# Expert 0 of a fused attention, MoE and cosine MLP kernel: its second token batch as seven block products, and attention's pair loads, score banks and operand sums arranged anew

## The chip, the cores and the metric

The kernel runs on one core of one Trainium2 chip. The metric is the device time of one execution in microseconds (us). Three runs of the kernel before gave 1342.14 (the median), 1338.18 and 1342.61. The trace comes from a further, profiled execution.

## The reference, cut to what matters

Three stages follow each other in float32. Sliding window attention (2 batches, 8 heads, 768 tokens, 64 per head; every token sees the last 128 tokens and the first 4) gives 1536 token rows of 512. Eight experts work on all of them, weighted by a Sinkhorn balanced gate. A last MLP of 2048 hidden columns has the activation h cos h.

```python
keep = is_sink | in_window                      # 4 sink tokens, window 128
a = softmax(where(keep, q @ k.T / 8, -1e9));  x = a @ v
P = exp(x @ w_gate - max)
for _ in range(8):
    P /= P.sum(1) + 1e-9;  P /= P.sum(0) + 1e-9;  P *= N / E
for e in range(8):
    out += P[:, e:e+1] * (maximum(x @ w1[e], 0) @ w2[e])
h = out @ w_in;  return (h * cos(h)) @ w_out
```

## The kernel before

Expert work is TensorE work on split numbers: every float32 operand is kept as two float16 parts, hi and lo, and a product is three matmuls (hi hi, hi lo, lo hi) that add up in one bank of PSUM. Expert e has a first product (512 to 1024 columns, then the rectification) and a second one (1024 to 512), for token batch 0 and then for batch 1. The weights of the first product lie in `W1O`, the token operands of batch b in `XO[b]`, the rectified hidden rows in `HH`, the weights of the second product in `W2S`, the token rows (attention's result, later the output) in `ACC[b]`.

The first product has two forms. The plain form, `g1_plain` (L1099), takes the blocks as they are: 192 matmuls of 384 columns a batch, one rectification for each of 16 results. The block form, `g1` with the list `CHAIN` (L1032), works on halves of tokens and of the inner dimension with seven products in place of eight (Strassen's scheme): 168 matmuls, results added together out of the banks by DVE. It needs seven operands instead of four: sums and differences of the four weight blocks (S, on POOL, L297 to L300, split by ACT and DVE into `W1O`) and of the four token blocks. Before the change expert 0 is plain in both batches. The token sums that experts 1 to 7 need are made by `sum_operands`: from the split operands in `XO[b]`, 14 DVE steps and 4 ACT steps, for batch 0 beside expert 0's first product of batch 1, for batch 1 beside expert 1's first product.

Attention works in units: a unit is one pair of heads, one tile of 128 tokens. In turn: `scores` (L579, PE), `top` (DVE takes the maximum and brings the scores out of the bank, L589), `expo` (ACT, L599), `high` (ACT, L622), `low` (POOL, L628), `turn` (a DMA transpose on SP's queue, L638), `values` (PE, L651 and L656), `norm` (DVE, L665 to L668). For batch 0 a pair's q and k come in two halves, q as two loads of 64 rows into a zero-filled tile, so that the score matmul has 128 rows in; batch 1 has whole pairs and matmuls of 64 rows. When the token rows are there, `plain_operand` splits them (ACT hi at L176, lo at L177 on POOL or DVE) into a staging tile `xs` and a DMA transpose on SP's queue (L221) carries them into `XO[b]`, eight pieces for each batch. For batch 1 the staging tiles are two buffers in turn (the tag "f64", `bufs=2`), which the weight sums S and pieces of w2 use too.

The order is written out by hand: `put(t, every, steps)` sets steps at ticks, `run(n)` and `tick()` issue them between matmuls. On every engine instructions run in that order. PSUM has eight banks, handed out as rings by name: s for scores, x for values, l for gates and sinks, L for the plain first product, g2 for the second product. Attention runs alone at first; from `start` its steps are laid between the matmuls of expert 0's first product of batch 0 (28 ticks, `GT`), and the rest between those of its second product (24 ticks, `HT_`). The rectification for expert 0 is `act_first` (ACT the hi part, DVE the lo part straight from the bank), for the others `act_relu` (two ACT steps, then POOL).

Of the kernel before, what the change touches and what calls it, by code (L numbers as in the profile page):

```python
# [40 lines left out]
def kernel(  # L41
# [123 lines left out]
    BW = ((1, 1, 0), (0, 1, 0), (1, 0, 0), (0, 1, 0))  # L165
# [119 lines left out]
    def w1_split(e, st, js=range(NJ)):  # L285

        steps = []
        for j in js:
# [15 lines left out]
            def sp(which, j=j, by=by, ca=ca, cb=cb):  # L304
# [19 lines left out]
        return steps  # L324
# [9 lines left out]
    def attention():  # L334
# [16 lines left out]
        q0 = [xo0[:, 7 * HT * c + 3 * HT:7 * HT * c + 5 * HT] for c in range(2)]  # L351
        wide = Ring(t.rearrange("p (h w) -> p h w", h=2) for t in (q1[:, 0], q1[:, 1], *q0))
        qs = Ring([TMP.rearrange("p a b -> p (a b)")[:, 4096:4096 + S], q1[:, 0], q1[:, 1]])
        for t in wide.parts:
            for g in range(2):
                nc.vector.memset(t[64 * g:64 * g + 64, 1 - g], 0.0)
        kk = carve(2 * NT * TW)
        few = Ring(kk[:, 4 * TW * n:4 * TW * (n + 1)].rearrange("p (t w) -> p t w", w=TW) for n in (1, 2, 0))
        ks = Ring(kk[:, NT * TW * n:NT * TW * (n + 1)].rearrange("p (t w) -> p t w", w=TW) for n in range(2))
        k_sink = res.tile([128, NP, NS], F32, name="ksink")  # L360
# [21 lines left out]
        def load_qk(n, eng=nc.scalar, other=nc.scalar):  # L382
            r = order[n % NP] * 128
            if n < 2 * NP:
                half = n // NP
                t0, nt = (2, 4) if half else (0, 3)
                qk[n] = q_, k_ = wide.next(), few.next()
                eng.dma_start(
                    out=k_[:, 0:nt, 0:128],
                    in_=kT[0, r:r + 128, t0 * 128:(t0 + nt) * 128].rearrange("p (t w) -> p t w", w=128))  # L390
                for g in range(2):
# [3 lines left out]
            else:  # L395
                qk[n] = q_, k_ = qs.next(), ks.next()
                eng.dma_start(
                    out=k_[:, :, 0:128], in_=kT[1, r:r + 128, :].rearrange("p (t w) -> p t w", w=128))
                other.dma_start(out=q_, in_=qT[1, r:r + 128, :])

        def sink_cols(n):
            k_ = qk[n][1]
            if n < NP:
                nc.gpsimd.tensor_copy(out=k_sink[:, n], in_=k_[:, 0, 0:NS])
            src = k_sink[:, n % NP:n % NP + 1] if n < 2 * NP else k_[:, 0:1, 0:NS]
            a, z = ((1, 2), (0, 3), (1, NT - 1))[n // NP]
            nc.gpsimd.tensor_copy(out=k_[:, a:z, 128:TW], in_=src.to_broadcast([128, z - a, NS]))
# [138 lines left out]
        for p in range(2 * NP):  # L546
            h, p = p // NP, p % NP
            for u in range(U3):
                i = h * U3 + u
                units.append((0, p, i))  # L550
                batch.append(h * NP + p)
                sums.append((slice(h * U3, h * U3 + U3), u, U3) if p < NP - 1 else (slice(i, i + 1), 0, 1))
        for p in range(NP):
# [4 lines left out]
            for g in groups:  # L558
                tiles = range(NT)[g]
                for u, i in enumerate(tiles):  # L560
                    units.append((1, p, i))
                    batch.append(2 * NP + p)
# [3 lines left out]
        def scores(k):  # L566
# [3 lines left out]
            qi, ki = (i % U3, i - 2 * (i // U3)) if k < KB else (i, i)  # L570
            S_[k] = []
            for ab in range(2):
                sps = ring["s"].next()
                h, qh = (slice(0, 128), q_[:, ab]) if k < KB else (slice(64 * ab, 64 * ab + 64), q_)
                if sunk(i):
                    to, kh = sps[:, 0:L], k_.rearrange("p t w -> p (t w)")[h, (ki - 1) * TW:(ki - 1) * TW + L]
                else:
                    to, kh = sps[:, 0:L].rearrange("p (t w) -> p t w", w=128), k_[h, 0:i + 1, 0:128]
                nc.tensor.matmul(to, qh[h, qi * 128:(qi + 1) * 128], kh, start=True, stop=True)  # L579
# [160 lines left out]
        first = [batch.index(n) for n in range(3 * NP)]  # L740
        for n, k in enumerate(first):
            put(base(k) - 2, 1, [lambda n=n: sink_cols(n)])
            if n >= 3:
                m = n - 3 if n < 2 * NP else n - 2
                put(base(first[m + 1] - 1) + 3, 1, [lambda n=n: load_qk(n)])

        def ops(b, half, c, tiles, s0):
            def go():
                if b:
                    xs = stage.tile([128, 1536], F16, tag="f64", name="xs", bufs=2)  # L750
                else:
                    xs = xss.next()
                plain_operand(b, half, c, tiles, xs, nc.vector if c else nc.gpsimd)
# [3 lines left out]
        ends = []  # L757
        for b in range(B):
            s0 = 0
            for half in range(2):  # L760
                for c in range(2):
                    for tiles in [slice(0, U3)] if c == 0 else [slice(i, i + 1) for i in range(U3)]:
                        i = half * U3 + tiles.stop - 1
# [585 lines left out]
```

## Time and profile before

| what | us |
|---|---|
| median of three runs | 1342.14 |
| profiled execution | 1342.73 |
| its span | 1340.8 |
| PE busy in the span | 1276.2 (95%) |
| attention alone | 0 to 69.6 |
| first product of expert 0, batch 0, with attention | 69.6 to 159.5 |
| second product of batch 0, with attention's tail | 159.5 to 198.3 |
| first, then second product of batch 1 | 198.3 to 231.8, to 265.0 |
| the rest | 265.0 to 1340.8 |

The stages are bounded by the start of the first matmul of each product. A row of stretches gives for one of them its length, then busy us and number of instructions of each engine; the clock is the mean share of full speed that was granted to TensorE; the DMA share is that of the 16 engines. A waits row says which engine's instruction waited for whose, in total, how often, and the longest. A group row has the idle time ahead of the group behind the bar.

### The profile page before, as it was taken

To read this page: it belongs to the slowest core of one execution; us is meant where nothing else is said; L and a number is where in the kernel's file an instruction comes from. 1 tells how busy PE (TensorE), PEld (TensorE's weight loads), DVE (VectorE), ACT (ScalarE), POOL (GpSimd) and SP (SyncE) were. 2 spreads that over 40 slices of the span, in tenths; PEclk is the share of its full clock that TensorE was granted. 3 is DMA by queue.
4 is the path that set the end of the run, shared out by engine and by line. 5 is a ranking of instruction groups with operands and counts; after the bars stand their busy time and mean duration, and the time that the engine had idled before them with its cause. 6 is when DMAs were issued, how large, how long until landed. Compare 5 with 4: busy or idle time off the path is not lost.

```text
span 1340.8 us, 19538 instructions
## 1 busy us (share of the span) xinstructions
PE 1276.2 (95%) x7281; PEld 682.7 (51%) x7281; DVE 855.3 (64%) x1636; ACT 681.3 (51%) x1425; POOL 596.9 (45%) x742
## 2 busy tenths in 40 slices
PE   5777999999999999999999999999999998999998
PEld 4544556454555545455554545545455544445554
DVE  6675517886557554754755485475556688787674
ACT  6755632473644437164443716445372757666452
POOL 5533412150633364173336417333541857377543
PEclk7789999999999999999999999999999999999999
DMA  9998660011112310501331050132102331400001
GB/s 241 164 177 157 134 144 2 2 66 64 59 64 88 116 64 17 187 1 63 98 107 64 24 181 1 63 103 102 63 25 86 56 104 28 104 2 0 32 17 48
DMA packets 127599, 104.57 MB, mean 78 GB/s; under 512 B 89104, under 2 KB 102928, under 8 KB 127504
## 3 DMA queue, kind: packets, MB, share of 16 engines
q1 hardware_dynamic: 112384, 72.57, 21.1%
q0 software_dynamic: 7168, 25.17, 5.8%
q10 hardware_dynamic: 7952, 5.59, 1.9%
q8 instruction: 57, 0.93, 0.3%
q14 instruction: 38, 0.31, 0.1%
HBM read 70.53 MB, written 11.53 MB: 61 GB/s over the span
## 4 chain that ended last, share of the span: by engine, by line
PE 69%; DVE 9%; POOL 4%; ACT 4%; issue 3%; DMA 1%; POOLq 0%; ACTq 0%; DVEq 0%
PE bank L1116 37%; PE bank L1032 25%; PE bank L1049 4%; PE bank L1099 2%; DVE tmp L1063 1%; DVE tmp L970 1%; DMA xo<-xs 1%; DVE w2s L183 1%; POOL hh L945 1%; DVE w1o L183 1%; DVE tmp L230 1%; DVE tmp L961 1%; ACT xs L182 1%; ACT tmp L958 1%; DVE xs L183 1%
## 5 line engine op out<-in xcount | busy, mean ns | idle before, releaser
L1116 PE MATMUL bank<-w2s,hh 128*128 128x512 f16 x2880 | 637.6, 379 | 4.7 <-DVE w2s L183 2.3
L1116 PEld LDWEIGHTS <-hh 128*128 128x128 f16 x2880 | 280.9, 98 | 337.9 <-issue 6.2
L1032 PE MATMUL bank<-xo,w1o 128*128 128x384 f16 x2352 | 386.2, 326 | 0.9 <-ACT tmp L1000 0.8
L945 POOL TENSOR_TENSOR hh<-tmp,hh 128x384 f16<-128x384 f32 x224 | 206.3, 942 | 328.2 <-ACT tmp L944 319.5
L1032 PEld LDWEIGHTS <-w1o 128*128 128x128 f16 x2352 | 229.5, 98 | 154.3 <-issue 2.0
L1000 ACT ACTIVATE tmp<-bank 128x384 f32<-128x384 f32 x168 | 81.6, 487 | 289.0 <-PE bank L1032 289.0
L1004 DVE TENSOR_TENSOR tmp<-bank,tmp 128x384 f32<-128x384 f32 x168 | 91.1, 554 | 163.9 <-ACT tmp L1000 121.8
L1049 PE MATMUL bank<-xo,w1o 128*128 128x384 f16 x672 | 120.0, 329 | 6.7 <-ACT tmp L1071 3.6
L1188 DVE SCALAR_TENSOR_TENSOR acc<-bank,PS,acc 128x512 f32<-128x512 f32 x84 | 62.9, 749 | 75.9 <-PE bank L1116 75.4
L1049 PEld LDWEIGHTS <-w1o 128*128 128x128 f16 x672 | 65.9, 98 | 57.9 <-issue 10.5
L944 ACT ACTIVATE tmp<-tmp 128x384 f32<-128x384 f32 x168 | 87.9, 523 | 5.3
L943 ACT ACTIVATE hh<-tmp 128x384 f16<-128x384 f32 x168 | 86.5, 515 | 5.1 <-DVE tmp L1004 5.0
L972 POOL TENSOR_SCALAR hh<-tmp 128x384 f16<-128x384 f32 x64 | 45.7, 715 | 82.8 <-DVE tmp L970 72.9
L160 DVE TENSOR_REDUCE wm<-st 128x1 f32<-128x1024 f32 x68 | 81.7, 1208 | 0.0
L628 POOL TENSOR_TENSOR parts<-xo,parts 128x512 f16<-128x512 f32 (+1 forms) x38 | 47.4, 1249 | 71.6 <-ACT parts L622 56.7
L182 ACT ACTIVATE w1o<-S,s 128x1024 f16<-128x1024 f32 x36 | 41.2, 1145 | 74.4 <-POOL S L300 74.4
L1099 PE MATMUL bank<-xo,w1o 128*128 128x384 f16 x384 | 73.3, 341 | 1.9 <-DVE hh L950 1.9
L183 DVE SCALAR_TENSOR_TENSOR w1o<-st,s,w1o 128x512 f16<-128x512 f32 x72 | 65.1, 935 | 13.5 <-ACT w1o L182 13.4
L974 POOL TENSOR_TENSOR hh<-tmp,hh 128x384 f16<-128x384 f32 x64 | 68.8, 1076 | 5.3
L183 DVE SCALAR_TENSOR_TENSOR w2s<-st,s,w2s 128x512 f16<-128x512 f32 x72 | 60.9, 860 | 15.6 <-ACT w2s L182 15.5
L1063 DVE TENSOR_TENSOR tmp<-bank,tmp 128x384 f32<-128x384 f32 x112 | 59.2, 548 | 10.9 <-PE bank L1049 6.9
L183 DVE SCALAR_TENSOR_TENSOR w1o<-S,s,w1o 128x1024 f16<-128x1024 f32 x36 | 49.4, 1373 | 19.1 <-ACT w1o L182 19.0
(181 smaller groups left out, 1361.1 us busy)
## 6 DMA issues: line engine op xcount, KB each, us to landing
st<-in_moe_w_dram SPq DMA_DIRECT2D x56, 512.0 KB, 5.9
f<-in_moe_w_in_dram POOLq DMA_DIRECT2D x16, 512.0 KB, 4.4
f<-in_moe_w_out_dram POOLq DMA_DIRECT2D x16, 512.0 KB, 4.2
w2p<-in_moe_w_dram SPq DMA_DIRECT2D x8, 512.0 KB, 4.4
w_in<-x POOLq DMA_DIRECT2D x16, 256.0 KB, 4.3
w_out<-x POOLq DMA_DIRECT2D x16, 256.0 KB, 4.1
st<-w_out SPq DMA_DIRECT2D x8, 512.0 KB, 5.9
st<-w_in SPq DMA_DIRECT2D x8, 512.0 KB, 6.9
```

What stands on the lines that cost most here:

```text
L160: nc.vector.tensor_reduce(out=dst, in_=src, axis=axis, op=ALU.max, apply_absolute_value=True)
L183: late.append(lambda: nc.vector.scalar_tensor_tensor(out=lo, in0=src, scalar=s, in1=hi, op0=ALU.mult, op1=ALU.subtract))
L943: nc.scalar.activation(out=hi, in_=src, func=AF.Relu)
L944: nc.scalar.activation(out=dst, in_=src, func=AF.Relu)
L945: nc.gpsimd.tensor_tensor(out=lo, in0=dst, in1=hi, op=ALU.subtract)
L1000: nc.scalar.activation(out=t, in_=ps, func=AF.Copy)
L1004: nc.vector.tensor_tensor(out=t, in0=ps, in1=t, op=ALU.add)
L1032: nc.tensor.matmul(ps, W1O[:, j0 + c, wi, o, kk, :], XO[b][:, kk, o, xi, :], start=(n == 0 and o in (0, 5, 1)), stop=(n == 5), skip_group_ ...
L1049: nc.tensor.matmul(ps, W1O[:, j, wi, o, kk, :], XO[b][:, kk, o, xi, :], start=(n == 0), stop=(n == 5))
L1063: nc.vector.tensor_tensor(out=t, in0=x, in1=y, op=ALU.add)
L1099: nc.tensor.matmul(ps, W1O[:, j, wi, o, kk, :], XO[b][:, kk, x, xi, :], start=(kk == 0 and m == 0 and p == 0), stop=(kk == 1 and m == 1 an ...
L1116: nc.tensor.matmul(ps, HH[:, t // U3, hi, f, (t % U3) * 128:(t % U3 + 1) * 128], w[:, wi, f, :], start=(f == order[0] and n == 0), stop=(f ...
```

## The change

The second batch of expert 0 takes the block form (`if e == b == 0` keeps the plain form for the first batch only). For that its token operands are made by `x_operand` in six pieces of 14 blocks each, with sums T on POOL, and expert 0's weight sums S are added in the second product of batch 0 (`put(GT + 1, 1.5, w1_rest[9:])`); `sum_operands(1)` goes, and `sum_operands(0)` moves there too. The rectification is `act_relu` throughout. Batch 0's pairs are loaded whole, all at the start, and have 64 row scores. From eight ticks ahead of the first product's start, scores have four banks, values and gates one each.

```diff
-    BW = ((1, 1, 0), (0, 1, 0), (1, 0, 0), (0, 1, 0))
+    BW = ((0, 0, 0),) * 4
...
-                elif e == 0:
+                elif e == 0 and which == 2:
                     split(hi[:, 3], lo[:, 3], t[:, 0:2, cb], s, by=by[2])
...
             steps += [lambda w=w, sp=sp: sp(w) for w in range(3)]
-        return steps
+            if e == 0:
+                rest += [sums, lambda sp=sp: sp(3)]
+        return steps + rest
...
-            if n < 2 * NP:
-                half = n // NP
-                t0, nt = (2, 4) if half else (0, 3)
-                qk[n] = q_, k_ = wide.next(), few.next()
...
-                for g in range(2):
-                    other.dma_start(
-                        out=q_[64 * g:64 * g + 64, g],
-                        in_=qT[0, r + 64 * g:r + 64 * g + 64, half * HT:(half + 1) * HT])
...
+            b, r = n // NP, order[n % NP] * 128
+            qk[n] = q_, k_ = qs[n], ks[n]
+            eng.dma_start(
+                out=k_[:, :, 0:128], in_=kT[b, r:r + 128, :].rearrange("p (t w) -> p t w", w=128))
+            other.dma_start(out=q_, in_=qT[b, r:r + 128, :])
...
+        for p in range(2, NP):
+            load_qk(p, nc.sync, nc.sync)
...
-                h, qh = (slice(0, 128), q_[:, ab]) if k < KB else (slice(64 * ab, 64 * ab + 64), q_)
+                h = slice(64 * ab, 64 * ab + 64)
...
-            ops = ((0, 0), (1, 2)) if i < U3 else ((5, 0), (6, 2))
+            ops = ((0, 0), (1, 2)) if i < U3 else ((6, 2), (0, 0), (3, 0)) if b else ((5, 0), (6, 2))
...
+        def sum_ops(c, i, s0):
+            box = []
+            put(s0, 1, [lambda: box.append(x_operand(1, c, i, None))])
+            put(s0 + 2, 1, [lambda: box.pop()()])
+
+        for c in range(2):
+            for i in range(U3):
+                last = KB + (2 * c + 2) * NT - 1 - (2 * (U3 - 1 - i) if c else 0)
+                s0 = max(s0 + 3, turned[last] + 2, base(len(units)) + 6)
+                sum_ops(c, i, s0)
...
-                banks(s=(0, 1))
+                banks(s=(0, 1, 5, 7), x=(4,), l=(6,))
...
-            if e == 0:
+            if e == b == 0:
                 for half in range(2):
                     g1_plain(b, half, act)
...
+        put(GT, 1, [lambda: banks(s=(0, 1, 2, 3))])
...
-        put(6, 1, w1_rest[6:])
-        pairs = [TMP[:, n:n + 2] for n in (9, 11)]
+        put(6, 1, w1_rest[6:9])
+        put(GT + 1, 1.5, w1_rest[9:])
+        ring["c"] = Ring(W1O[:, j, wi, 4:7].rearrange("p a k w -> p (a k w)").bitcast(F32) for j in range(NJ) for wi in range(2))
+        a = ACC[0].rearrange("p t c -> p (t c)")
+        put(GT + 1, 0.75, sum_operands(0, ...))
...
-                    put(4, 2.5, sum_operands(0, *pairs))
-                if e == 1 and not b:
-                    banks(A0=(2,), A1=(3,), B0=(6,), B1=(0,), C=(1,))
-                    put(2, 2.5, sum_operands(1, *pairs))
+                    banks(A0=(2,), A1=(3,), B0=(6,), B1=(0,), C=(1,), l=(5,))
+                    ring["c"] = Ring(TMP[:, n] for n in range(9))
                 so = None
-                act = act_relu if e else act_first
+                act = act_relu
```

`x_operand(b, c, i, s)`, which the last MLP uses already, makes one piece (token tile i of both halves, every second block of columns from c):

```python
T  = stage.tile([128, 4, 128], F32, tag="z", name="T")
xs = stage.tile([128, 7, 2, 128], F16, tag="f64", name="xs", bufs=2)
g.tensor_tensor(out=T[:, 1::2], in0=x[:, 1], in1=x[:, :, 0], op=ALU.subtract)   # POOL, L197
g.tensor_tensor(out=T[:, 2], in0=x[:, 1, 1], in1=T[:, 1], op=ALU.subtract)      # L198
g.tensor_tensor(out=T[:, 0], in0=x[:, 0, 1], in1=T[:, 2], op=ALU.subtract)      # L199
split(xs[:, 0:2, 0], xs[:, 0:2, 1], x[:, 0], s)                                 # ACT hi, DVE lo
split(xs[:, 6, 0], xs[:, 6, 1], x[:, 1, 1], s)
# two steps later: ACT hi and POOL lo of T into xs[:, 2:6], then the DMA transpose of xs into XO[b]
```

On POOL, the second product of expert 0's batch 0 ended like this before: the last low parts of attention (`parts`), two low parts of token pieces (`xs`), and then the weight sums of expert 1.

```order
L628 TENSOR_TENSOR parts_111<-xo1_70,parts_111 128x512
L631 TENSOR_TENSOR parts_111<-xo1_70,parts_111 128x8
L177 TENSOR_TENSOR xs_2062<-acc1_75,xs_2062 128x2x384
L177 TENSOR_TENSOR xs_2166<-acc1_75,xs_2166 128x2x384
L297 TENSOR_TENSOR S_2655<-st_2219 128x256
```

Now the same stage has between two low parts of token pieces the sums T of a later piece, and here the four instructions of one of expert 0's weight sums.

```order
L177 TENSOR_TENSOR xs_2137<-T_2136,xs_2137 128x4x128
L197 TENSOR_TENSOR T_2179<-acc1_75 128x2x128
L198 TENSOR_TENSOR T_2179<-acc1_75,T_2179 128x128
L199 TENSOR_TENSOR T_2179<-acc1_75,T_2179 128x128
L297 TENSOR_TENSOR S_2188<-tmp_77 128x256
L298 TENSOR_TENSOR S_2188<-S_2188,tmp_77 128x256
L299 TENSOR_TENSOR S_2188<-tmp_77 128x256
L300 TENSOR_TENSOR S_2188<-tmp_77,S_2188 128x256
L177 TENSOR_TENSOR xs_2180<-T_2179,xs_2180 128x4x128
L197 TENSOR_TENSOR T_2200<-acc1_75 128x2x128
```

The third low part (`xs_2180`) stands behind the fourth sum S (`S_2188`); the numbers at the names tell one tile of a buffer from the next. On ACT, in the same stage, before: the hi parts of the eight pieces (L176), and the copies of the second product's results out of the banks (L1183).

```order
L176 ACTIVATE xs_2062<-acc1_75 128x2x384
L1183 ACTIVATE acc0_74<-bank7_85 128x512
L176 ACTIVATE xs_2097<-acc1_75 128x2x128
L176 ACTIVATE xs_2121<-acc1_75 128x2x128
L176 ACTIVATE xs_2149<-acc1_75 128x2x128
L1183 ACTIVATE acc0_74<-bank5_83 128x512
L176 ACTIVATE xs_2166<-acc1_75 128x2x384
L176 ACTIVATE xs_2176<-acc1_75 128x2x128
L176 ACTIVATE xs_2183<-acc1_75 128x2x128
L176 ACTIVATE xs_2190<-acc1_75 128x2x128
L1183 ACTIVATE acc0_74<-bank7_85 128x512
```

Now, for the last three pieces:

```order
L176 ACTIVATE xs_2201<-acc1_75 128x2x128
L176 ACTIVATE xs_2201<-acc1_75 128x128
L182 ACTIVATE w1o_71<-S_2188,s_422 128x1024
L1168 ACTIVATE acc0_74<-bank5_83 128x512
L176 ACTIVATE xs_2201<-T_2200 128x4x128
L176 ACTIVATE xs_2237<-acc1_75 128x2x128
L176 ACTIVATE xs_2237<-acc1_75 128x128
L241 ACTIVATE xo0_69<-acc0_74 128x2x384
L176 ACTIVATE xs_2237<-T_2236 128x4x128
L176 ACTIVATE xs_2257<-acc1_75 128x2x128
L176 ACTIVATE xs_2257<-acc1_75 128x128
L1168 ACTIVATE acc0_74<-bank7_85 128x512
```

Each piece has three hi parts instead of one, and the copies out of the banks (now L1168) stand between those of one piece and the next. On SP's queue the start was this before, with q and k of batch 0 in halves:

```order
L392 DMA xo_70<-in_q_dram 64x384 x2
L411 DMA acc_75<-in_v_dram 128x6x128
L388 DMA xo_70<-in_k_dram 128x3x128
L392 DMA xo_70<-in_q_dram 64x384 x2
L411 DMA acc_75<-in_v_dram 128x6x128
L388 DMA xo_70<-in_k_dram 128x3x128
L392 DMA xo_69<-in_q_dram 64x384 x2
L411 DMA acc_75<-in_v_dram 128x6x128 x2
L268 DMA tmp<-in_moe_w_dram 128x1024 x2
L638 DMA_TRANSPOSE parts<-parts 128x4x128
```

Now:

```order
L385 DMA xo_70<-in_q_dram 128x768
L394 DMA acc_75<-in_v_dram 128x6x128 x2
L383 DMA xo_70<-in_k_dram 128x6x128
L385 DMA xo_70<-in_q_dram 128x768
L394 DMA acc_75<-in_v_dram 128x6x128 x2
L383 DMA xo_69<-in_k_dram 128x6x128
L385 DMA xo_69<-in_q_dram 128x768
L383 DMA xo_69<-in_k_dram 128x6x128
L385 DMA xo_69<-in_q_dram 128x768
L268 DMA tmp<-in_moe_w_dram 128x1024 x2
L621 DMA_TRANSPOSE parts<-parts 128x4x128
```

All four pairs stand whole ahead of expert 0's w1 (`tmp`) and of attention's first transpose.

## Rows read from the trace of the kernel before

**Rows 1.** Stretches: length, busy of PE, PEld, DVE, ACT, POOL, clock, DMA, GB/s.
```profile
0.00:69.60 69.60, 44.17 (x293) 34.02 (x294) 43.57 (x171) 48.88 (x137) 36.73 (x91) 0.75 1.02 200
69.60:159.50 89.90, 70.43 (x654) 42.66 (x653) 56.03 (x176) 51.30 (x141) 35.03 (x44) 0.91 0.82 165
159.50:198.30 38.80, 38.00 (x276) 19.21 (x274) 10.93 (x35) 15.11 (x35) 10.74 (x11) 1.00 0.57 114
198.30:231.80 33.50, 33.39 (x268) 20.84 (x266) 22.04 (x37) 9.79 (x19) 6.90 (x8) 1.00 0.07 28
231.80:265.00 33.20, 32.32 (x160) 15.41 (x158) 28.98 (x83) 12.19 (x19) 5.67 (x8) 1.00 0.00 1
265.00:1340.80 1075.80, 1057.88 (x5639) 550.59 (x5637) 693.77 (x1136) 544.06 (x1075) 501.84 (x580) 1.00 0.21 65
```

**Rows 2.** Waits, 69.6 to 159.5: us in total, times, longest.
```profile
PE bank L579 <- DVE mx L589: 10.3, 5, 2.9
...
ACT parts L622 <- DMA parts<-parts: 7.1, 2, 3.7
...
PE bank L656 <- DVE acc L668: 4.0, 2, 2.1
```

**Rows 3.** Groups by line and form, DVE, 69.6 to 159.5.
```profile
L950 DVE SCALAR_TENSOR_TENSOR hh<-bank,hh 128x384 f16<-128x384 f32 x15 | 8.3, 554 | 15.1 <-ACT hh L949 15.0
```

**Rows 4.** The timeline of PE, scores: start, us, engine, line.
```profile
66.60 1.12 PE L579 MATMUL bank<-xo,xo 128*128 128x260 f32 x4
...
166.20 0.71 PE L579 MATMUL bank<-xo,tmp 64*128 64x260 f32 x4
```

**Rows 5.** DMA issues: times, KB each, median us to landing.
```profile
xo<-xs SPq DMA_TRANSPOSE x20, 4.0
```

**Rows 6.** The timeline of POOL, ACT and PE, 173 to 200.
```profile
172.27 1.16 POOL L628 TENSOR_TENSOR parts<-xo,parts 128x512 f16<-128x512 f32 x1 [0.29 <-ACT parts L622]
...
189.94 0.94 ACT L176 ACTIVATE xs<-acc 128x256 f16<-128x256 f32 x2 [4.26 <-DMA xo<-xs]
190.79 0.58 ACT L1183 ACTIVATE acc<-bank 128x512 f32<-128x512 f32 x1
...
198.15 1.14 PE L1099 MATMUL bank<-xo,w1o 128*128 128x384 f16 x6
199.12 0.45 PE L681 MATMUL bank<-wg,xo 128*128 128x8 f16 x12
```

**Rows 7.** Groups by line and form, first 370 us.
```profile
L182 ACT ACTIVATE w1o<-S,s 128x1024 f16<-128x1024 f32 x6 | 6.8, 1136 | 0.0
...
L298 POOL TENSOR_TENSOR S<-S,st 128x256 f32<-128x256 f32 x7 | 5.7, 819 | 0.5
L300 POOL TENSOR_TENSOR S<-st,S 128x256 f32<-128x256 f32 x6 | 5.6, 926 | 0.0
L297 POOL TENSOR_TENSOR S<-st 128x256 f32<-128x256 f32 x7 | 5.5, 786 | 61.7 <-DVE cr L836 41.4 <-DMA st<-in_moe_w_dram 17.4 <-DVE w1o L183 2.8
...
L299 POOL TENSOR_TENSOR S<-st 128x256 f32<-128x256 f32 x7 | 5.1, 724 | 0.0
```

**Rows 8.** Groups by line and form, whole span.
```profile
L197 POOL TENSOR_TENSOR T<-acc 128x256 f32<-128x256 f32 x12 | 10.5, 873 | 11.2 <-DVE acc L1188 6.9 <-DVE xs L183 4.2
...
L182 ACT ACTIVATE xs<-T,s 128x512 f16<-128x512 f32 x12 | 8.6, 715 | 7.8 <-POOL T L199 7.8
...
L198 POOL TENSOR_TENSOR T<-acc,T 128x128 f32<-128x128 f32 x12 | 6.4, 536 | 0.9
...
L199 POOL TENSOR_TENSOR T<-acc,T 128x128 f32<-128x128 f32 x12 | 5.8, 486 | 0.9
```

**Rows 9.** The timeline of DVE and POOL.
```profile
203.85 1.20 DVE L230 TENSOR_TENSOR tmp<-xo 128x768 f32<-128x768 f16 x1
...
204.31 1.32 POOL L298 TENSOR_TENSOR S<-S,st 128x256 f32<-128x256 f32 x1
...
208.47 0.73 POOL L298 TENSOR_TENSOR S<-S,st 128x256 f32<-128x256 f32 x1
```

More of the change, by code (lines that the diff above doesn't have):

```diff
@@ L285, in w1_split @@
     def w1_split(e, st, js=range(NJ)):
-        steps = []
+        steps, rest = [], []
         for j in js:
@@ L739, in attention @@
                 put(turned[k] + 1, 1, [lambda k=k: norm(k)])
-        first = [batch.index(n) for n in range(3 * NP)]
-        for n, k in enumerate(first):
+        for n in range(B * NP):
+            k = batch.index(n)
             put(base(k) - 2, 1, [lambda n=n: sink_cols(n)])
[L743 to L747, printed above, removed]
+            if n >= NP:
+                free = max(j for j, m in enumerate(batch) if m == (n - NP if n < NP + 2 else n - 2))
+                put(base(free) + 3, 1, [lambda n=n: load_qk(n)])
@@ L748, in go, with ops @@
+        def ops(half, c, tiles, s0):
             def go():
[L749 to L753, printed above, removed]
-            put(s0, 1, [go])
[L757 to L763, printed above, removed]
-                        last = units.index((b, 2 * c + 1, i))
-                        s0 = max(s0 + 2, turned[last] + 2, base(len(units)) + 6 if b else 0)
-                        ops(b, half, c, tiles, s0)
-                ends.append(s0 + 4)
+                plain_operand(0, half, c, tiles, xss.next(), nc.vector if c else nc.gpsimd)
+            put(s0, 1, [go])
@@ new lines, in attention @@
+        ends, s0 = [], 0
+        for half in range(2):
+            for c in range(2):
+                for tiles in [slice(0, U3)] if c == 0 else [slice(i, i + 1) for i in range(U3)]:
+                    last = units.index((0, 2 * c + 1, half * U3 + tiles.stop - 1))
+                    s0 = max(s0 + 2, turned[last] + 2)
+                    ops(half, c, tiles, s0)
+            ends.append(s0 + 4)
+        def sum_ops(c, i, s0):
+            box = []
+            put(s0, 1, [lambda: box.append(x_operand(1, c, i, None))])
+            put(s0 + 2, 1, [lambda: box.pop()()])
@@ L768, in attention @@
+        for c in range(2):
+            for i in range(U3):
+                last = KB + (2 * c + 2) * NT - 1 - (2 * (U3 - 1 - i) if c else 0)
+                s0 = max(s0 + 3, turned[last] + 2, base(len(units)) + 6)
+                sum_ops(c, i, s0)
+        ends.append(s0 + 5)
         st = {}
@@ L797, in attention @@
             if n == ends[0] - 8:
-                banks(s=(0, 1))
+                banks(s=(0, 1, 5, 7), x=(4,), l=(6,))
             run(n)
-        steps = [lambda n=n: run(n) for n in range(start, ends[3])]
+        steps = [lambda n=n: run(n) for n in range(start, ends[2])]
         k = max(0, ends[1] - 8 - start)
         def less(f=steps[k]):
-            banks(x=(4,), l=(6,))
             a16s.parts[3:] = []
@@ L945, in act_relu @@
             nc.gpsimd.tensor_tensor(out=lo, in0=dst, in1=hi, op=ALU.subtract)
-        def act_first(src, ft, half):
-            hi, lo = (HH[:, half, hl, ft] for hl in range(2))
-            nc.scalar.activation(out=hi, in_=src, func=AF.Relu)
-            nc.vector.scalar_tensor_tensor(out=lo, in0=src, scalar=0.0, in1=hi, op0=ALU.max, op1=ALU.subtract)
         def act_cos(src, ft, half, sc):
@@ L1105, in g1_plain @@
                         tick()
-                pend.append((None, lambda ps=ps, f=NJ * high + j: act(ps, f, half)))
+                pend.append((None, lambda ps=ps, f=NJ * high + j: act(ps, f, half, ring["c"].next())))
         orders = ([0, NJ, 1, NJ + 1, NJ + 2, NJ + 3, 2, 3], [f for j in range(NJ) for f in (j, NJ + j)])
@@ L1170, in layers @@
                 late = order[-1:]
-            for t in tiles if 0 < e < E else range(NT):
+            for t in tiles if 0 < e + b and e < E else range(NT):
                 if t in ps:
```

63 lines of the change are left out of this document (24 added, 39 removed).

## The prediction, made before the changed kernel ran

> **What bounds the kernel now.** I read the stretches first [rows 1]. There the reader is to set PE's busy time against the length of each stage. From 159.5 us on PE is hardly ever idle: 38.00 of 38.80, 33.39 of 33.50, 32.32 of 33.20, then 1057.88 of 1075.80. There only fewer or shorter matmuls help, or a new wait hurts. Ahead of that attention sets the pace. In the first stage PE is busy for 44.17 of 69.60 us, its clock is 0.75 of full, and the DMA engines have a share of 1.02, so nothing more fits into them. In the second, PE is busy for 70.43 of 89.90 us, at 0.91. So the change can win in the first two stages and by matmuls that go, and it can lose where the third stage hands over to the fourth.
>
> The waits of the second stage [rows 2] then show what ends PE's idle time: the score banks that DVE has not read out yet (10.3 us in 5 waits) and the value bank (4.0 us in 2). ACT's hi parts wait 7.1 us for transposes out of the tiles that they are to write, in 2 waits. The last views were groups and timelines, for prices.
>
> **The change part by part.** A, the start. 24 units of batch 0 get score matmuls with 64 rows in: a unit took 1.12 us for four matmuls with 128 rows and 0.71 with 64, both in stretches of full clock [rows 4]. If every one were on the path, 24 x 0.41 = 9.8 us would go. The memsets of DVE and five of ACT's groups of load issues go too. Against this, all four pairs now stand ahead of expert 0's w1 and the first transpose on SP's queue. With tiles of 128x768 float32 (0.39 MB), six halves of pairs move ahead there by some 1.7 MB in all; at the stage's 200 GB/s [rows 1] that is 8.6 us during which a queue that is already full serves loads which nobody needs yet. As the bytes of the whole stage are about the same and the DMA share is 1.02, I take a gain of 3 us, from -10 to +6.
>
> The Trainium skill (TensorE: Matmul & The Clock Gate, Part 3: Packing small matmuls) says that matmuls in different row groups of the array run beside each other, so a pair of 64-row score matmuls should cost about what one does, 1.12/2 = 0.56 us. The trace has 0.71, some of the way [rows 4]; by the page's rule A would be 24 x 0.15 = 3.6 us better at most.
>
> B, the first product of batch 0. Four score banks remove most of the 10.3 us [rows 2], and about half of it reappears at the next thing that is late: the transposes for which ACT already waits 7.1 us. That is -5. The single value bank can add what that wait is now, 4.0 again; as the values come later than DVE's steps I take +3. DVE loses the lo parts of the rectification, 15 x 554 ns = 8.3 us [rows 3], which were in the same queue as the score steps: -3. ACT gets a second rectification each time and POOL the subtraction; both have room (51.30 and 35.03 of 89.90). A clock of 0.91 over 89.9 us means 2 x 0.09 x 89.9 = 16 us at the lower of its two levels (1.2 of 2.4 GHz), in which 8 us are lost; with fewer holes I take -3 of these. Together -8, from -15 (all of the 10.3, the 3 and some of the clock) to 0.
>
> C, the second product of batch 0: here I see the cost. G is the start of this stage, 159.5. Before, POOL's last low part of attention ends at 173.43, G + 13.9 [rows 6]. Now POOL has these ahead of the first piece's low part: two weight sums S between attention's low parts (each four instructions, 786 + 819 + 724 + 926 ns = 3.25 us [rows 7]), of whose 6.5 us I let half vanish in POOL's idle time (it is busy for 10.74 of 38.80 [rows 1]); the sum T (873 + 536 + 486 ns = 1.9 us [rows 8]); a third S, 3.25; and the low part itself, 1.16 like the row at 172.27. So the first piece is staged at G + 13.9 + 3.2 + 1.9 + 3.25 + 1.16 = G + 23.4.
>
> From there a chain runs through two buffers: xs and S use one tag with two buffers in turn (S0, xs0, xs1, S3, xs4 in one; S1, S2, xs2, xs3, xs5 in the other, in the order in which the program asks for them). Whoever takes a buffer in which an xs lay waits until its transpose has landed, 4.0 us (20 of them, median [rows 5]). Before, eight pieces went through the same two buffers, but without S and with one hi step of ACT each; the row at 189.94 shows ACT waiting 4.26 us for just such a landing. Now the steps are: xs0 lands, 4.0. Then the hi parts of xs1 (0.94/2 = 0.47 for 256 columns and half of that for 128, 0.71), the hi part of S2 that stands between (1.14 [rows 7]), that of T (0.72 [rows 8]), the low part on POOL (1.16): 3.7. xs1 lands, 4.0. S3 may then start, and POOL has the low part of xs2 behind it: 3.25 + 1.16 = 4.4. xs2 lands, 4.0. xs3: 0.71, the hi part of S3 1.14, a copy out of a bank 0.58 [rows 6], T 0.72, low 1.16: 4.3. It lands, 4.0. xs5, which needs xs3's buffer: 0.71 + 0.58 + 0.72 + 1.16 = 3.2, and 4.0 to land. The sum is 5 x 4.0 + 15.6 = 35.6 us, so `XO[1]` is whole at G + 59.0. The block product of batch 1 starts with a product that needs all three tiles and both column blocks, so PE can begin it only there. Before it began at 198.15, G + 38.7 [rows 6]. PE waits 20 us.
>
> The bounds: if the waits for landings overlap with the work entirely, POOL alone sets it: five further pieces of 1.9 + 1.16, S3's 3.25 and one landing after G + 23.4, which is G + 45.9; with all of S0 to S2 in idle time 3 less, some +4 us. Above, every low part and sum by a quarter longer beside DVE's steps gives +26. I take +20, because each step of the chain is an order that the program fixes.
>
> What is queued behind: the copies out of banks 5 and 7 stand on ACT between the hi parts, so the second product's last two tiles wait for banks too; that lies inside the same 20 us. After so long a hole PE begins again at the lower clock: the first two stages, with their holes, are those with a clock under 1 [rows 1]. I take +1.5, from 0 to 3.
>
> D, matmuls. 192 become 168 in the first product of batch 1. Six took 0.97 us from 198.15 to 199.12 [rows 6], so 24 save 24 x 0.162 = 3.9. Gates of three tiles take 18 more small ones, 0.45/12 each, 0.7. -3.2, with little doubt: from 231.8 on the block form already runs back to back.
>
> E, operand sums. Those of batch 1 leave expert 1, those of batch 0 leave expert 0's batch 1; in the stretch 231.80 to 265.00 PE had 0.88 us idle [rows 1] and DVE was busy for 28.98. I take -2, from -3 to 0. That is what they cost now; in their new place DVE is busy for 10.93 of 38.80, and 14 steps of about 1.2 us [rows 9] go in.
>
> The sum on the profiled execution, 1342.7 (its span is 1340.8): -3 - 8 + 20 + 1.5 - 3.2 - 2 = +5.3, so 1348. This execution lies 0.6 above the median of the three runs, which are 4.4 apart; I leave it at that. A difference of 0.3%, 4 us, is about what can be told from no change.
>
> **The rivals.** R1, the chain is no chain: S and the transposes overlap, the buffers turn at POOL's pace. Then C is +4 and there is no clock to win back: -3 - 8 + 4 - 3.2 - 2 = -12, so 1331. It decides from the point where a landing holds the next piece up by under 1 us instead of 4. For it: POOL is idle most of the stage. Against it: the row at 189.94, where ACT waited for a landing with the same two buffers.
>
> R2, slower by more: attention gains nothing, since DMA sets the first stage and the pairs ahead of w1 delay it. It decides when the first transpose leaves over 5 us later than before. A is +4, B -1, the rest as forecast: 4 - 1 + 20 + 1.5 - 3.2 - 2 = +19, so 1362. For it the DMA share of 1.02 [rows 1]; against it that bytes only move within the stage.
>
> R3, DVE holds POOL up. A sum on POOL took 1.32 us while DVE's 1.20 us step with two operands from SBUF ran, and 0.73 us without [rows 9]. In C 14 such DVE steps now run beside some 22 of POOL's steps; if eight on the chain lose 0.6 each it is 5 us more, 1353. The Trainium skill (SBUF — State Buffer, Who interferes with whom) has this as a rule: the two engines share one pair of ports, and one that loses waits for the other's whole instruction. The trace agrees, with 0.6 us.
>
> R4, half of the chain holds: C is +11, 1339. A variant between forecast and R1, if the program's buffers turn in another order than I read.
>
> **How the numbers follow.** The forecast 1348, with 1340 to 1357 for its own unknowns (B alone has 7 us each way), has 0.45. R1 has 0.22, R2 0.13, R3 0.10, R4 0.10. From 1330 to 1360 holds R1's centre, R3, R4 and nearly all of the forecast; a part of R1 below and of R2 above is left out, 2 in 10. Faster than 1338.1: R1, 0.22, a third of R4 and 0.03 of the forecast, 0.29. Slower than 1346.2: R2 and R3, 0.23, and 0.31 of the forecast, 0.54. The rest, 0.17, is within 0.3%.
>
> **What would show it.** A: the first matmul of expert 0 (69.6 before) some us earlier, and the first transpose not over 5 us later. B: 82 us from there to the second product, few waits for score banks. C: a hole of PE ahead of batch 1's first block product of 15 to 25 us, ended by transposes of xs, with POOL's S3 and ACT's hi parts waiting for landings of about 4 us one after the other. D: the first product of batch 1 takes 30 instead of 33.5 us. If the hole is under 8 us the forecast is wrong in C, and the time lies near R1; if the first stage is not shorter, A and R2 decide.

## The result, and the profile after

The changed kernel took 1356.79 us (median of five runs, 1354.04 to 1357.2), against 1340.17 for the kernel before in the same session; the ratio is 1.0109, interval 1.0097 to 1.0121. It is slower: by 14.6 us by the ratio, which is not the quotient of these two medians, and by 16.6 us as the medians stand. The forecast was 1348, with a range from 1330 to 1360.

The stretches of the profile after, cut at the same places (columns as in [rows 1]):

```profile
0.00:67.71 67.71, 38.32 (x295) 22.79 (x295) 40.78 (x166) 50.31 (x140) 35.84 (x84) 0.81 1.00 229
67.71:154.66 86.95, 67.90 (x656) 40.82 (x654) 48.31 (x158) 56.83 (x157) 44.91 (x59) 0.89 0.73 146
154.66:218.44 63.78, 40.91 (x273) 19.50 (x272) 36.86 (x58) 25.40 (x54) 45.89 (x51) 0.87 0.37 68
218.44:250.24 31.80, 29.95 (x261) 18.88 (x260) 13.51 (x25) 18.25 (x41) 10.51 (x12) 1.00 0.26 79
250.24:282.68 32.44, 32.36 (x162) 15.66 (x160) 25.13 (x77) 13.10 (x23) 15.19 (x21) 1.00 0.00 1
282.68:1355.10 1072.42, 1057.62 (x5638) 550.50 (x5636) 678.73 (x1121) 541.04 (x1071) 499.35 (x580) 1.00 0.21 66
```

Against [rows 1] the stages moved by -1.9, -3.0, +25.0, -1.7, -0.8 and -3.4 us, together 14.3, the difference of the spans (1355.1 - 1340.8). The loss stands in the third row alone, the second product of batch 0: PE's busy time grew by 3, its stage by 25, POOL's work there from 10.74 to 45.89 and the clock fell to 0.87. PE's idle times over 0.5 us in that stage and the first in the next, by the timeline:

```profile
157.73 0.27 PE L634 MATMUL bank<-w2s,parts 128*128 128x130 f16 x2 [0.97 <-DVE acc L651]
...
168.78 0.49 PE L639 MATMUL bank<-w2s,parts 128*128 128x65 f16 x6 [5.38 <-DVE acc L651]
...
206.26 6.81 PE L1101 MATMUL bank<-w2s,hh 128*128 128x512 f16 x24 [15.99 <-ACT acc L1168]
...
220.95 0.65 PE L1017 MATMUL bank<-xo,w1o 128*128 128x384 f16 x3 [1.85 <-DMA xo<-xs]
```

The hole of 16 us ends with ACT's copy out of a bank, the last one of 1.85 with the landing of the last piece. The wait of 5.4 us ahead of the hole is for the single value bank. Why ACT is late is read off its timeline, here from the first landing on (the lines with L176 and `xs` are the hi parts of pieces):

```profile
187.89 0.62 ACT L176 ACTIVATE xs<-acc 128x256 f16<-128x256 f32 x2 [8.40 <-DMA xo<-xs]
188.41 1.13 ACT L182 ACTIVATE w1o<-S,s 128x1024 f16<-128x1024 f32 x1
189.45 0.61 ACT L176 ACTIVATE xs<-T 128x512 f16<-128x512 f32 x1
...
204.08 0.61 ACT L176 ACTIVATE xs<-acc 128x256 f16<-128x256 f32 x2 [8.22 <-DMA xo<-xs]
204.60 1.13 ACT L182 ACTIVATE w1o<-S,s 128x1024 f16<-128x1024 f32 x1
205.64 0.57 ACT L1168 ACTIVATE acc<-bank 128x512 f32<-128x512 f32 x1
```

and off POOL's:

```profile
181.94 1.87 POOL L177 TENSOR_TENSOR xs<-T,xs 128x512 f16<-128x512 f32 x1
...
190.14 1.73 POOL L177 TENSOR_TENSOR xs<-T,xs 128x512 f16<-128x512 f32 x1 [3.87 <-ACT xs L176]
...
196.00 0.72 POOL L297 TENSOR_TENSOR S<-tmp 128x256 f32<-128x256 f32 x1 [0.81 <-DVE acc L230]
...
198.84 1.15 POOL L177 TENSOR_TENSOR xs<-T,xs 128x512 f16<-128x512 f32 x1
...
206.81 1.25 POOL L177 TENSOR_TENSOR xs<-T,xs 128x512 f16<-128x512 f32 x1 [4.94 <-ACT xs L176]
...
211.86 1.16 POOL L177 TENSOR_TENSOR xs<-T,xs 128x512 f16<-128x512 f32 x1 [0.74 <-ACT xs L176]
...
215.70 1.16 POOL L177 TENSOR_TENSOR xs<-T,xs 128x512 f16<-128x512 f32 x1 [0.74 <-ACT xs L176]
```

These rows show the forecast chain step by step. The low parts end at 183.8, 191.9, 200.0, 208.1, 213.0 and 216.9. About 4 us behind the first (187.89) ACT may write xs1; S3 begins at 196.00, 4.1 behind the second, though the profile names for its last 0.81 us a sum on DVE that ended then; xs3's hi part stands at 204.08, 4.1 behind the third. These are three rounds of 8.1 us, each a landing and the work behind it. The landing behind the fourth low part holds ACT up for only 0.33 us more: the last two pieces, 5.0 and 3.8 us after the one before, come at the pace of the work on POOL and ACT. The copy at 205.64, which PE waits for, is queued behind xs3's hi part on ACT. From the first low part's end to the last landing, 220.8, it is 37.0 us.

### The profile page after: what moved, and what is told of

It is laid out like the page before. It is cut to its first block, busy times and chain, and to the rows that moved or that the text cites. A ratio compares the mean times of both kernels' runs of the same rounds, so it can differ in the third digit from the quotient of the medians.

```text
span 1355.1 us, 19599 instructions
## 1 busy us (share of the span) xinstructions
PE 1267.0 (94%) x7275; PEld 668.1 (49%) x7275; DVE 843.3 (62%) x1604; ACT 704.9 (52%) x1482; POOL 651.7 (48%) x804
## 4 chain that ended last, share of the span: by engine, by line
PE 68%; DVE 7%; POOL 6%; issue 4%; ACT 4%; DMA 2%; POOLq 0%; ACTq 0%; DVEq 0%
PE bank L1101 36%; PE bank L1017 28%; PE bank L1034 4%; DMA xo<-xs 2%; DVE tmp L1048 2%; POOL hh L935 1%; DVE tmp L955 1%; DVE w1o L183 1%; DVE tmp L946 1%; POOL S L300 1%; DVE acc L230 1%; POOL parts L611 1%; ACT xs L182 1%; POOL S L298 1%; POOL T L197 1%
## 5 line engine op out<-in xcount | busy, mean ns | idle before, releaser
L1101 PE MATMUL bank<-w2s,hh 128*128 128x512 f16 x2880 | 640.4, 380 | 18.8 <-ACT acc L1168 16.2
L1017 PE MATMUL bank<-xo,w1o 128*128 128x384 f16 x2520 | 414.5, 326 | 2.5 <-DMA xo<-xs 1.9
L935 POOL TENSOR_TENSOR hh<-tmp,hh 128x384 f16<-128x384 f32 x240 | 217.9, 929 | 350.7 <-ACT tmp L934 348.4
L1017 PEld LDWEIGHTS <-w1o 128*128 128x128 f16 x2520 | 245.4, 98 | 165.7 <-issue 3.3
L985 ACT ACTIVATE tmp<-bank 128x384 f32<-128x384 f32 x180 | 87.7, 488 | 301.6 <-PE bank L1017 301.5
L989 DVE TENSOR_TENSOR tmp<-bank,tmp 128x384 f32<-128x384 f32 x180 | 97.6, 554 | 175.4 <-ACT tmp L985 130.4
L1034 PE MATMUL bank<-xo,w1o 128*128 128x384 f16 x672 | 120.4, 329 | 6.6 <-ACT tmp L1056 3.7
L934 ACT ACTIVATE tmp<-tmp 128x384 f32<-128x384 f32 x180 | 94.1, 523 | 5.7
L1034 PEld LDWEIGHTS <-w1o 128*128 128x128 f16 x672 | 66.1, 99 | 58.0 <-issue 10.8
L933 ACT ACTIVATE hh<-tmp 128x384 f16<-128x384 f32 x180 | 92.6, 515 | 1.8 <-DVE tmp L989 1.6
L182 ACT ACTIVATE w1o<-S,s 128x1024 f16<-128x1024 f32 x40 | 45.8, 1145 | 74.7 <-POOL S L300 74.6
L183 DVE SCALAR_TENSOR_TENSOR w1o<-st,s,w1o 128x512 f16<-128x512 f32 x72 | 65.2, 937 | 14.0 <-ACT w1o L182 13.9
L959 POOL TENSOR_TENSOR hh<-tmp,hh 128x384 f16<-128x384 f32 x64 | 68.8, 1075 | 5.3
L183 DVE SCALAR_TENSOR_TENSOR w1o<-S,s,w1o 128x1024 f16<-128x1024 f32 x40 | 54.4, 1360 | 22.5 <-ACT w1o L182 22.5
L1048 DVE TENSOR_TENSOR tmp<-bank,tmp 128x384 f32<-128x384 f32 x112 | 59.2, 548 | 10.8 <-PE bank L1034 6.7
L951 ACT ACTIVATE tmp<-tmp,scl 128x384 f32<-128x384 f32 x64 | 39.1, 610 | 26.9 <-DVE tmp L946 26.9
```

Source lines behind the costliest of these rows:

```text
L183: late.append(lambda: nc.vector.scalar_tensor_tensor(out=lo, in0=src, scalar=s, in1=hi, op0=ALU.mult, op1=ALU.subtract))
L933: nc.scalar.activation(out=hi, in_=src, func=AF.Relu)
L934: nc.scalar.activation(out=dst, in_=src, func=AF.Relu)
L935: nc.gpsimd.tensor_tensor(out=lo, in0=dst, in1=hi, op=ALU.subtract)
L959: nc.gpsimd.tensor_tensor(out=lo, in0=k, in1=hi, op=ALU.subtract)
L985: nc.scalar.activation(out=t, in_=ps, func=AF.Copy)
```

## The experiments

G is again the start of the second product of batch 0 in each profile, and "whole" is the landing of the last piece. Each experiment has the name of its run in brackets. They come from three sessions, and each ratio is to the kernel before in the same one: its median was 1341.46 for s_first, third_buffer, sums_back and two_value_banks, 1341.37 for both, both_two_T, plain_b1 and plain_dve, 1342.59 for old_banks and the three with spread. Executions of one kernel lie 3 to 8 us apart, so the length of a stage in one profile is no measure of a difference of a few us.

**The order of S (s_first).**

```diff
-        put(GT + 1, 1.5, w1_rest[9:])
+        put(GT + 1, 0.5, w1_rest[9:])
```

> One number changed in the changed kernel: expert 0's weight sums S come every 0.5 ticks instead of every 1.5, so that all four stand on POOL ahead of the first token piece xs0. The work is the same, only its order changes. Theory (a chain through two buffers that xs and S share, 4 us for every landing): xs0 is staged some 3 us later, but from there pieces go in pairs, xs2 waits for xs0 only, xs4 for xs2, and no S stands between them. XO[1] is whole near 207 instead of 220.8 us, PE's hole of 16 us shrinks to 3 or less, time near 1344. Rival (POOL simply has too much to do in this stage): the same instructions end at the same time, 1356, within 2. Rival (DVE's sums hold POOL up): no change either.

Measured: 1351.4, ratio 1.0076 (1.006 to 1.0091). ACT's hi parts wait for landings for 1.4 us in all, instead of 17.0, and from the first piece to the last landing it is 28.0 us instead of 37.0. Not all of these 9 us were waits for buffers: the work of S3, 2.9 us on POOL, stood in the chain and now stands ahead of it. And the first piece is staged at G + 35.7 instead of G + 29.2, and a new wait stands ahead of it:

```profile
PE bank L639 <- DVE acc L651: 15.1, 2, 12.0
...
DVE w1o L183 <- ACT w1o L182: 10.6, 4, 4.3
...
ACT xs L176 <- DMA xo<-xs: 1.4, 2, 0.7
```

DVE's low parts of S wait in its queue for ACT, which waits for POOL's sums; behind them stands the step that empties the single value bank, and PE waits 12 us for that. The time fell by 5 us where the theory said 13. The stage itself is 63.2 us in this profile, against 63.8: the hole of 16 us fell to 3.2, and the waits for the value bank took its place. So the theory is right on the chain and wrong on the time.

**A third buffer (third_buffer).** Pieces xs0, xs2 and xs4 go to the end of `TMP`.

```diff
+            if b == 1 and s is None and (3 * c + i) % 2 == 0:
+                xs = TMP.rearrange("p a b -> p (a b)")[:, 4096:4992].bitcast(F16)...
```

> The changed kernel with a third staging buffer: pieces xs0, xs2 and xs4 go into the end of TMP that the last q tile leaves free, the others and S keep the two shared buffers. Order on every engine as in the changed kernel. Theory (chain through two buffers): xs1 and S3 no longer wait for a landing; five landings in a row become three, XO[1] whole near 205 instead of 220.8, time near 1342. Rival (POOL's load): the stage ends with POOL's last low part as now, 1356 within 2. Rival (DVE's sums hold POOL up): no change.

Measured: 1349.78, ratio 1.0059 (1.0042 to 1.0077). The stage is 56.6 instead of 63.8 us, the next one 33.9 instead of 31.8 (at a clock of 0.95); whole at G + 59.5 instead of G + 66.2. Here the order is unchanged and only the buffer is new: of the 6.7 us the chain behind the first piece gives 5.0, and the first piece is staged 1.7 earlier. ACT waits for no landing any more. It is half of the expected gain: with the landings gone POOL sets the pace, and its sums T take up to 3.4 us a piece where [rows 8] have 1.9.

**Sums back (sums_back).** `sum_operands(0)` goes back to `put(T0 + 4, 2.5, ...)` with its tiles in `TMP`.

> The changed kernel with batch 0's operand sums (14 DVE steps, 4 ACT steps) back beside expert 0's first product of batch 1, every 2.5 ticks. Theory of the chain: three or four of POOL's steps on the chain lose the 0.5 to 0.9 us by which they are stretched now, and no ACT step of the sums stands between the pieces; the hole is 2 to 4 us shorter, the next stage up to 1 longer: 1354. Rival (DVE's sums are the cause of the hole): the hole is 8 us shorter or more, 1348 or less. If nothing moves (1356 within 2), the stretched steps are covered by landings.

Measured: 1351.94, ratio 1.0081 (1.0063 to 1.0099). The first piece is staged at G + 23.4, where the prediction put it, against G + 29.2; the chain behind it takes 36.0, the stage 58.8 us, and the second product of batch 1, which has DVE's sums beside it again, 35.1 instead of 32.4. The interval of the ratio still touches that of the changed kernel. S3 waits for a landing here too, with no sum on DVE, and begins 4.1 us behind the second low part:

```profile
187.19 0.72 POOL L297 TENSOR_TENSOR S<-tmp 128x256 f32<-128x256 f32 x1 [2.17 <-DMA xo<-xs]
```

POOL beside DVE's sums, in the changed kernel:

```profile
179.85 0.73 POOL L299 TENSOR_TENSOR S<-tmp 128x256 f32<-128x256 f32 x1
179.95 1.44 DVE L230 TENSOR_TENSOR xo<-acc,xo 128x768 f16<-128x768 f32 x1
180.53 1.45 POOL L300 TENSOR_TENSOR S<-tmp,S 128x256 f32<-128x256 f32 x1
181.42 1.36 DVE L230 TENSOR_TENSOR acc<-xo,acc 128x768 f32<-128x768 f16 x1
```

and the same two steps and the low part behind them without:

```profile
172.49 0.73 POOL L299 TENSOR_TENSOR S<-tmp 128x256 f32<-128x256 f32 x1
173.17 0.73 POOL L300 TENSOR_TENSOR S<-tmp,S 128x256 f32<-128x256 f32 x1
173.85 1.16 POOL L177 TENSOR_TENSOR xs<-T,xs 128x512 f16<-128x512 f32 x1
```

The low part was 1.87 there. PE's hole stays (13.79 us, ended by the same copy), so DVE's sums are a part of the loss and not the cause of the hole.

**Two value banks (two_value_banks).** `banks(s=(0, 1, 5), x=(4, 7), l=(6,))`, then `s=(0, 1, 2), x=(4, 3)`.

> The changed kernel with two banks for values and three for scores in place of one and four (from the first product on s = 0, 1, 5 and x = 4, 7; from the second s = 0, 1, 2 and x = 4, 3). Theory (the single value bank eats what the score banks gave): PE's three waits of 6.5, 1.0 and 5.4 us for DVE's reading of the value bank go, attention ends 5 to 8 us earlier, and as the chain of pieces starts with attention's last rows all of it moves up: 1349, within 3. Rival (those waits only move to the score banks or the transposes): 1356 within 3.

Measured: 1353.93, ratio 1.0094 (1.0078 to 1.011), whose interval overlaps that of the changed kernel. The waits for the value bank went, the hole grew to 19.6 us, and the stage stayed at 63.7: the chain of pieces ends the stage anyway.

**Both (both)**, the third buffer and the sums back.

> third_buffer and sums_back together in the changed kernel. Theory (landings, and DVE's sums beside POOL, are the two parts of the loss and add up): the first piece is staged at G + 23.4 as in sums_back, from there POOL's own work sets the pace with T 1.7, the wait for the hi part 0.7 and the low part 1.15 for each of five pieces, S3 2.9, a landing 4.0: XO[1] whole at G + 48 instead of G + 59 (sums_back) or G + 60 (third_buffer), time near 1341. Rival (one of the two hides the other): 1350, as each alone.

Measured: 1342.76, ratio 1.0006 (0.9994 to 1.0019). The two add up: 14.0 us by the medians, where one alone gave 7.0 and the other 4.9. Whole at G + 50.8, PE's largest idle time in the stage 3.3 us.

**Two tiles for T, low parts on DVE (both_two_T).**

```diff
-            T = stage.tile([128, 4, 128], F32, tag="z", name="T")
+            T = stage.tile([128, 4, 128], F32, tag="x", name="T", bufs=2)
...
-            put(s0, 1, [lambda: box.append(x_operand(1, c, i, None))])
+            put(s0, 1, [lambda: box.append(x_operand(1, c, i, None, gl=nc.vector))])
```

> As both, with two tiles for the sums T in place of one and the low parts of T on DVE, which is idle there. Theory (POOL waiting for ACT between T and the low part is what is left): POOL has only sums, a piece costs it 1.7, XO[1] is whole near G + 42 and PE's hole is under 5 us; time near 1335, faster than both kernels. Rival (the transposes on one queue, or attention's last rows, are next): not over 3 us better than both.

Measured: 1334.92, ratio 0.9942 (0.9928 to 0.9955), faster than the kernel before and than the changed one. Whole at G + 44.1; there is no hole at the hand-over (3.3 us for the value bank are PE's longest wait in the stage), the third stage has 44.46 us with PE busy for 39.45 at a clock of 0.96:

```profile
150.84:195.30 44.46, 39.45 (x275) 19.14 (x273) 25.89 (x50) 22.14 (x50) 35.24 (x45) 0.96 0.60 109
225.08:260.13 35.05, 32.86 (x161) 15.46 (x159) 32.50 (x85) 14.56 (x25) 17.98 (x22) 1.00 0.00 0
```

The second row is where the operand sums went: DVE is busy for 32.50 of 35.05 us, and the stage is 2.6 us longer than in the changed kernel. Two things changed at once, the second tile for T and the engine of the low parts; no run parts them.

**Only the second batch back (plain_b1)** to the plain form, all else as changed.

> The changed kernel with only expert 0's second batch put back: plain form, token pieces, operand sums of both batches and weight sums as before; whole pairs, 64 row scores, banks and act_relu stay as changed. It shows A and B alone. Theory (A and B gain, C loses): the two attention stages are 8 us shorter together, the rest as before: 1333, within 3. Rival (the rearranged attention gains nothing that lasts, its end is set by the same late rows): 1341, within 2.

Measured: 1334.84, ratio 0.9936 (0.9913 to 0.996). A and B are worth 0.64% together, 8.6 us by the ratio and 6.5 by the medians; the block form as built here costs the rest of the way to 1356.8, some 22 us. And both_two_T, with the block form repaired, has 1334.92: the same time as this kernel, which does without it. Stage by stage both_two_T has 3.4 us less in the first product of batch 1 and 3.5 less from expert 1 on, but 6.7 more in the second product of batch 0 and 1.5 more in that of batch 1. So its gain over the kernel before is no more than what A and B give.

**The old rectification in that kernel (plain_dve)**, `act_first` for expert 0.

> As plain_b1, and the rectification of expert 0 is again ACT's hi part and DVE's lo part straight from the bank. It tests the term of B by which 8.3 us of DVE's time bring 3. Theory: 3 us slower than plain_b1, with more waits of the score banks. Rival (POOL and ACT, which take the work over, are as late as DVE was): within 1.5 of plain_b1, or faster.

Measured: 1339.02, ratio 0.9985 (0.9972 to 0.9999). The first product of batch 0 with the new rectification, then with the old one:

```profile
67.10:155.24 88.14, 69.35 (x655) 41.34 (x654) 48.41 (x158) 57.81 (x159) 45.92 (x59) 0.88 0.77 149
```

```profile
67.00:159.59 92.59, 70.67 (x656) 41.55 (x655) 54.56 (x173) 52.35 (x144) 35.20 (x44) 0.87 0.71 142
```

With the new rectification DVE has 6 us less to do and ACT and POOL have more, and the stage is 4.5 us shorter in these profiles. The intervals of the two ratios do not overlap, so the theory holds: the old rectification is slower.

**The old banks in that kernel (old_banks).**

> As plain_b1, with the banks for scores, values and gates as before the change (two for scores, two for values until late). It tests the largest term of B by itself: four score banks remove 10.3 us of waits of which 5 stay gone, a single value bank gives 3 back. Theory: 2 us slower than plain_b1, 1337. Rival (what the score banks give is eaten by the value bank and the transposes): within 1.5 of plain_b1. Rival (the single value bank costs more than four score banks bring): 2 us faster or more.

Measured: 1332.99, ratio 0.9934 (0.9913 to 0.9954). By the ratio that is plain_b1's time (0.9936), by the medians 1.9 us less; with four executions of each the three outcomes cannot be told apart for certain. With two score banks PE waits for them for 3.8 us, in the stage where [rows 2] had 10.3:

```profile
PE bank L560 <- DVE mx L570: 3.8, 5, 1.2
```

With four score banks it does not wait for them there at all, neither in plain_b1 nor in plain_dve, where DVE has its old work. But in plain_dve these stand in their place, for the one bank of the gates and the one of the values:

```profile
PE bank L662 <- DVE w2s L495: 4.9, 3, 2.7
PE bank L637 <- DVE acc L649: 4.7, 2, 2.6
```

So four banks do end the waits for score banks, and lighter work on DVE with two banks ends most of them; but where the new banks leave one each for values and gates, PE waits for DVE there instead. All of PE's waits for DVE in that stage come to 19.2 us before the change, 17.0 in plain_dve, 13.9 in plain_b1 and 9.3 with the old banks, each in one profile.

**The sums at another pace, and value banks again (spread, spread_values, spread_values_all)**, on top of both_two_T: `put(T0 + 2, 1.5, sum_operands(0, ...))`, then the two changes of banks.

> As both_two_T, with batch 0's operand sums from T0 + 2 every 1.5 ticks instead of from T0 + 4 every 2.5, so that they are done before the gate's normalizing steps, for which PE waits 2.2 us behind DVE. Theory: the second product of batch 1 is 2 us shorter, 1333. Rival (DVE's additions of the block products are then late): 1335 or more.

> As spread, with two value banks and three score banks from the second product of batch 0 on (s = 0, 1, 2 and x = 4, 3). Theory: PE's waits of 1.0 and 3.4 us for the value bank in that stage go, 3 us shorter than spread, 1330. Rival (attention's tail is then held by scores or transposes): within 1.5 of spread.

> As spread_values, and in the first product of batch 0 too three score banks and two value banks (s = 0, 1, 5 and x = 4, 7). Theory: that stage's value bank waits of 2 us each go as well, another 1 to 3 us, 1328. Rival (a score bank lost costs as much): as spread_values, within 1.5.

Measured: 1336.9, 1336.98 and 1338.11, ratios 0.9962 (0.9949 to 0.9975), 0.9966 (0.9953 to 0.9979) and 0.9963 (0.9951 to 0.9974); each time the rival came. The second product of batch 1 is shorter as expected, 33.7 instead of 35.0, but the first has 32.0 where both_two_T has 29.8: PE is idle for 1.8 us there instead of 0, 1.3 of them for ACT's copies of block products, which stand in ACT's queue behind a step that waits 3.1 us for DVE. The value banks bring nothing here either: in spread_values 3.7 us of waits for one go, and PE waits 4.6 for a copy of ACT instead.

## Why the prediction was right, and where it was not

**The size.** The forecast added up to +5.3 us, the profiles differ by 14.3. Term by term, forecast and measured: A -3 and -1.9, B -8 and -3.0, C with its clock +21.5 and +25.0, D -3.2 and -1.7, E -2 and -4.2. So the change is slower for the reason given, and the time is within the range, but 9 us above the middle: 5 of them are gains of B that did not come in this profile, 3.5 are C, and the rest nearly cancels.

**C was right in its mechanism and short in its size.** The forecast had the hole of PE, its cause, the order of its steps and its place. What was missing is R3, which had a chance of 0.10 and a price of 5: without DVE's sums beside POOL the first piece is staged at G + 23.4, as worked out, with them at G + 29.2, so 5.8 us, and the chain behind it takes 36.0 or 37.0, where the sum of steps said 35.6. With the sums back the last piece lands at G + 59.3, where that sum said G + 59.0. That it fits so closely is in part luck: attention's last low part ends at G + 16.2 there instead of the 17.1 taken, and T takes 2.9 instead of 1.9; and the last wait for a landing, taken at 4.0, is 1.5 there and 0.3 in the changed kernel, while the fifth piece, for which the sum had no step, takes 3.8 and 5.0. R3 is no alternative to the forecast but a term that belonged in its sum: the change itself put the 14 steps of [rows 9]'s kind beside POOL's chain. Most of the 5.8 us are POOL's steps stretched by 0.6 to 1.0 us; 2.1 are a wait of S2 for DVE, whose low part of an earlier S stood in its queue behind a wait for PE and one of the sums. The Trainium skill (SBUF — State Buffer, Who interferes with whom) calls the ports that the two engines share an exclusive lock, for which a DVE instruction with two inputs from SBUF contends with a POOL one that reads SBUF. The trace agrees, with 0.7 us lost at each of the two steps shown.

That the buffers are the cause is shown by the third buffer, which leaves every order and every instruction as it was and makes `XO[1]` whole 6.7 us earlier; the order of S, with fewer landings in a row too, takes 9 us from the chain. They also show what the forecast had not seen: under the landings lies a second chain, POOL's T, ACT's hi part and POOL's low part through one tile T, some 4.6 us a piece in s_first and 3.8 without DVE's sums (both). With the buffer and DVE's sums out of the way (both) PE still waits 2.5 and 2.4 us at the hand-over; with that chain opened as well (both_two_T) it does not. R1's price of 1331 supposed POOL's pace of 3.06 a piece, and a buffer alone gave 1349.8.

**A and B** were -3 and -8; by plain_b1 they are -8.6 together, by its ratio. The parts were mixed: A measured -0.9 to -2.8 in the thirteen profiles with the new start. In B the rectification, forecast at -3, is worth 4 us by the medians (by the ratios over 6); the score banks, forecast at -5, and the value bank, at +3, are worth nothing together that the runs can tell. The step that failed is that only half of the waits for score banks comes back, and at the transposes. In plain_dve, which has the banks and A but the old rectification, those waits are gone and the ratio is 0.9985, 2.0 us, no more than A's stage gives: PE waited for DVE at the banks of the values and the gates, where one each was left. What gained was the work taken off DVE. A's rival R2 (slower start) did not come: the first transpose leaves 3.3 us later (14.15 instead of 10.86), under the 5 that it needed, and the first product begins at 67.7, not later.

**D and E.** The first product of batch 1 is 1.7 us shorter, with 1.85 of waiting for the last piece in it; without that 3.5, against 3.2 forecast. E was -2 and measured -0.8 - 3.4 = -4.2: expert 1, too, runs shorter without its sums (59.0 instead of 62.3 us to the start of expert 2, with PE's waits of 2.3 us for the splitting of w2 on DVE gone). But the price of the place they went to, which the forecast named and did not add, is the 5.8 above.

**What stays open.** In profiles with the same orders up to there the first product of batch 0 took 83.7 us (s_first, third_buffer, sums_back, both_two_T) or 87 to 90 (the changed kernel, both, spread). In the longer ones one wait is longer, at the same place: 6.3 to 6.8 us instead of 2.0 to 3.3; in the changed kernel and in s_first:

```profile
139.16 0.38 PE L634 MATMUL bank<-w2s,parts 128*128 128x130 f16 x2 [6.49 <-DVE acc L651]
```

```profile
136.55 0.27 PE L634 MATMUL bank<-w2s,parts 128*128 128x130 f16 x2 [1.96 <-DVE acc L651]
```

What tips it was not found. B's -3.0 in the changed kernel's profile holds such a long stage, so B is rather judged by plain_b1. Which of the two changes of both_two_T counts is open, and so is how much of the waiting at the value bank is the single bank and how much is DVE's queue.

## What to carry to other kernels

When work is moved into a stage, list which buffers it takes in turn with what is there already, and follow one buffer from owner to owner: the time from a write to the landing of the transfer that reads it counts each time the turn comes round. A chain of waits hides the next one; price what lies under it before promising what its removal brings. Banks given to one ring are taken from another, and the wait can come up again there: before and after, add up all waits for the engine that empties them, and see what else stands in its queue. And compare a repaired kernel with one that leaves the feature out, not only with the one that the feature spoiled.

## What the hardware showed that was not expected

POOL's steps of 0.73 us took 1.45, and one of 1.16 took 1.87, while DVE ran steps with two operands from SBUF one after the other. DVE's own steps were stretched too: the difference of 128x768 into `xo` took 0.95 us at 192.80, where POOL's step beside it (0.46 us alone) took 1.25, and 1.44 at 179.95.
